# Two of six row groups of a small matrix no longer go through memory

## The chip, the cores and the metric

The kernel runs on one core of a Trainium2 chip. The metric is the device time of one execution in microseconds, the median over several runs.

## The reference

Two kinds of layer alternate, twice each, over an activation `x` of 2048 rows and 640 columns, all in fp32. The first kind is linear attention with 32 heads of 20 columns, the second a dense block with a squared ReLU:

```
qkv = layernorm(x) @ wqkv                       # 640 x 1920
phi(t) = where(t > 0, t + 1, exp(t)) + 1e-6
kv  = einsum("bhsd,bhse->bhde", phi(k), v);  z = sum over s of phi(k)
o   = einsum("bhqd,bhde->bhqe", phi(q), kv) / (einsum("bhqd,bhd->bhq", phi(q), z) + 1e-6)
x   = x + o @ wo
x   = x + relu(layernorm(x) @ w1 + b1)**2 @ w2 + b2     # 640 -> 1728 -> 640
```

## The kernel before

The order of all work on all engines is written out by hand; each engine executes its instructions in that order and waits on semaphores where data is missing. fp32 products are made from three passes over a high and a low half (`split`: ScalarE writes the high half, VectorE the difference), written for the matmuls in the type that the profile shows as fp32r.

A layer has three stages. In the first, the 16 tiles of 128 rows are normalised, transposed and projected to k and q (`part`, matmuls at L416), and G = normalised x times phi(k) is summed up over the tiles. For some tiles the q projection is left over as "late" parts: halves of 320 columns, each 15 matmuls, an exponential on ScalarE (L516) and two operations on VectorE (L523, L524). `late_q(n)` issues n of them. They serve as work for TensorE while other things are made ready.

In the second, short stage, which the change touches, a matrix M of 640 x 640 is made that joins kv and wo, so that the attention's output is phi(q) / den times M. `kv_make` forms the masked block-diagonal kv in six groups of 120 rows (the last of 40). `m_make(c)` multiplies group c by its rows of wo (L967) into a pair of PSUM banks (4, 6 and 2 in turn, from the list `mb`), lets ScalarE copy the 120 x 640 result to a tile `Mc` (L973), and sends that from ScalarE's own DMA queue to a matrix `md` in memory (L974).

M's rows are needed in another order: VectorE transposes q in 32 x 32 blocks only, which leaves the columns of a tile interleaved, and M's rows have to match. Row r of `md`, with r = 160 j + 32 m + b (j below 4, m below 5, b below 32), goes to partition 32 j + b of slice m. Three tiles `m_raw` (named `Mr` in the profile) hold slices 0 and 1, 2 and 3, and 4. `m_read(j, i)` fetches the part of row block j that belongs to tile i, one DMA on SyncE's queue (L979). The table `M_READ` says after which group which reads stand in SyncE's queue: block 0 after group 3, blocks 1 and 2 after group 4, block 3 after group 5. `m_split(m)` then makes the high half of slice m on ScalarE (L1008) and the low half on VectorE (L1009), in the tiles `uM`.

DMAs take eight completion counters in turn, over both issuing queues, so that a DMA is issued only when the one eight before it has landed.

Around this: while the groups are made, VectorE prepares tiles 1 to 3 of phi(q) (`b_step`), and `run_side` takes the next piece from a list of side work, here the splits of these tiles (`b_split`, L145 and L146). After the groups come three late parts, the splits of slices 0 and 1, one side piece, the split of slice 2, a fourth late part, the splits of slices 3 and 4. `proj` (L437) then makes the outputs of the first two tiles: slices 0 to 2 for both, then slices 3 and 4 for both, then tiles 2 and 3. `b_x1` adds the residual on VectorE (L694). SyncE, behind the reads, stores the late parts of phi(q) and loads the first weights of the third stage (L323), the dense block, interleaved with the attention's outputs for the remaining tiles.

Of the kernel before, what the change touches and what calls it, by code (L numbers as in the profile page):

```python
# [10 lines left out]
AF = mybir.ActivationFunctionType  # L11
# [6 lines left out]
DC = D // P  # L18
# [5 lines left out]
B32 = 32  # L24
# [6 lines left out]
NH = -(-D // HR)  # L31
# [21 lines left out]
def fast(b):  # L53
# [13 lines left out]
STAY = 1  # L67
FB0 = 0
KV_STEPS = (0, 1, 1, 1, 1, 0)
M_READ = {  # L70
    3: [(0, i) for i in range(3)],
    4: [(j, i) for i in range(3) for j in (1, 2)],
    5: [(3, i) for i in range(3)],
}
LOW_AT = 1
OUTS = (
# [6 lines left out]
def head_rows(c):  # L83
    return min(HR, D - HR * c)
# [3 lines left out]
def kernel(  # L88
# [11 lines left out]
    nc = tc.nc  # L100
# [13 lines left out]
    def bank(i, n=1):  # L114
        return PS[:, 512 * i : 512 * (i + n)]
# [23 lines left out]
    def ftile(name):  # L139
        return tmp.tile([P, D], F32, tag="f", name=name, bufs=F_BUFS)  # L140
# [265 lines left out]
    def halves(ps):  # L406
        return ps.rearrange("p (b n) -> p b n", b=2)[:, :, :HD]

    def halves_sb(t):
        return t.rearrange("p (b n) -> p b n", b=2)  # L410
# [60 lines left out]
    for layer in range(N_LAYERS):  # L471
# [3 lines left out]
        md = dram.tile([D, D], F32, name=f"md_{layer}", tag="md")  # L475
# [23 lines left out]
        def part(t, a, b, ps=None):  # L499

            ps = (xbank() if ps is None else ps)[:, : b - a]
            for c in range(DC):
                mm3(
                    ps, xT[t][:, 0, c, :], xT[t][:, 1, c, :],
                    kq[c][:, 0, a:b], kq[c][:, 1, a:b], c == 0, c == DC - 1,
                )
            return ps
# [23 lines left out]
        def xtile(name, dtype=R32):  # L531
            return xp.tile([P, 2, D], dtype, tag="x", name=name, bufs=8)
# [23 lines left out]
        if layer == 0:  # L556
# [21 lines left out]
            for ps, a, b in runs:  # L578
# [4 lines left out]
                d = T4[0][:, 0, 0, a * P : b * P]  # L583
                nc.scalar.activation(d, ps[:, : (b - a) * P], AF.Copy)
            first_loads.low(1)
            for ps, a, b in runs:
                d = T4[0][:, 0, :, a * P : b * P]
# [53 lines left out]
        def b_load_x(t):  # L641
            xr[t] = ftile("xr")
            nc.sync.dma_start(xr[t], src[t])
# [31 lines left out]
        def b_step(t, n=1):  # L675
            for _ in range(n):
                next(b_gen.setdefault(t, b_ops(t)), None)
# [7 lines left out]
        def b_split(t, u):  # L685
            split(u[:, 0], u[:, 1], yzp.pop(t))
            pT[t] = chunks(u)
# [51 lines left out]
        for t in range(NT):  # L739
# [66 lines left out]
            ps = ps_first if layer == 0 and t == 1 else part(t, 0, n0, bank(XB[0]))  # L806
# [12 lines left out]
            ps = part(t, n0, D if is_late else 1024, bank(XB[1]))  # L819
# [31 lines left out]
            else:  # L851
                ps = part(t, 1024, 2 * D, bank(XB[2]))
# [21 lines left out]
        def late_q(n=1, rest=True):  # L874

            for _ in range(n):
                if not late_parts:
                    return
                t, j = late_parts.pop(0)
                if j == 0:  # L880
                    late_phi[t] = Phi(ftile("rl"))
                late_phi[t].exp(j * HD, part(t, D + j * HD, D + (j + 1) * HD))
                late_todo.append((t, j))
                if rest:
                    late_rest()
# [21 lines left out]
        for j in range(JB):  # L907
            p, k = slice(j * B32, (j + 1) * B32), j % 2
# [25 lines left out]
        def run_side(n=1):  # L934
            for _ in range(min(n, len(side_work))):
                side_work.pop(0)()
# [3 lines left out]
        u = xtile("kvbd", F32).rearrange("p j n -> p (j n)")  # L940
# [16 lines left out]
                    )  # L957
            nc.vector.tensor_tensor(out=kvbd[c][:n, :n], in0=ps[:n, :n], in1=maskf[:n, :n], op=ALU.mult)

        mb = [4, 6, 2]  # L960

        def m_make(c):
            mb.append(mb.pop(0))
            ps = bank(mb[-1], 2)
            n, o = head_rows(c), HR * c
            for j in range(2):
                nc.tensor.matmul(  # L967
                    ps[:n, j * 512 : j * 512 + HD], kvbd[c][:n, :n],
                    vo["o", c][:n, j * HD : (j + 1) * HD], start=True, stop=True,
                )  # L970

            u = ftile("Mc")
            nc.scalar.activation(halves_sb(u[:n]), halves(ps[:n]), AF.Copy)  # L973
            nc.scalar.dma_start(md[o : o + n], u[:n])  # L974

        def m_read(j, i):

            w = min(2, DC - 2 * i)
            nc.sync.dma_start(  # L979
                m_raw[i][j * B32 : (j + 1) * B32, :w],  # L980
                md[j * R_ + 2 * i * B32 : j * R_ + (2 * i + w) * B32].rearrange(
                    "(m b) n -> b m n", b=B32
                ),
            )
# [21 lines left out]
        def m_split(m):  # L1006
            v = m_raw[m // 2][:, m % 2]
            nc.scalar.activation(M[m][:, 0], v, AF.Copy)  # L1008
            nc.vector.tensor_tensor(  # L1009
                out=M[m][:, 1], in0=v, in1=M[m][:, 0].bitcast(F32), op=ALU.subtract  # L1010
            )

        for c in range(NH):
# [5 lines left out]
            if c == 3:  # L1019
                b_load_x(1)  # L1020
            if KV_STEPS[c]:
                b_step(1, KV_STEPS[c])
        side_work.append(lambda: b_split(1, xtile("pT")))
# [8 lines left out]
        m_raw = [xtile("Mr", F32) for _ in range(3)]  # L1032
        side_work.append(lambda: b_split(2, xtile("pT")))
        Q = (3, 1, 1, 1)
        xbanks = [0, 1, 2, 3]
        for c in range(NH):
            m_make(c)
            b_step(2)
            for j, i in M_READ.get(c, ()):
                m_read(j, i)  # L1040
            if c > 3:
                run_side(1)
            if c > 0:
                b_step(3)
        side_work.append(lambda: b_split(3, xtile("pT")))
        late_q(Q[0])
        for m in range(2):
            m_split(m)
        run_side(1)
        m_split(2)  # L1050
        late_q(1)
        m_split(3)
        m_split(4)
# [89 lines left out]
        def fc1(g, c, spare=False):  # L1143
            if spare:
                ps = fresh("po0")
            elif g == 0 and c == 1:
                ps = fresh("po0")
            else:
                ps = fresh("h")
            u = wu.get(g, "w1", c)  # L1150
            xhi, xlo = xTb[g][:, 0], xTb[g][:, 1]
            if c == 13:
                w = u.rearrange("p (d f) -> p d f", d=DC)
                seq = [(w, xlo), (w, xhi)]
            else:
                w, wl = (u[:, j * D : (j + 1) * D].rearrange("p (d f) -> p d f", d=DC) for j in range(2))
                seq = [(w, xlo), (wl, xhi), (w, xhi)]
            order = [(d, a, bb) for d in range(DC) for a, bb in seq]
            if g == 0 and c == 0:

                order = [(d, a, bb) for a, bb in (seq[1], seq[2], seq[0]) for d in range(DC)]
            for n, (d, a, bb) in enumerate(order):
                nc.tensor.matmul(  # L1163
                    ps, a[:, d, :], bb[:, d, :], start=n == 0, stop=n == len(order) - 1
                )
            wu.used(g, "w1", c)
            return ps
# [425 lines left out]
        for g in range(NG):  # L1593
            for c in range(NF):
                ps = fc1(g, c)
# [63 lines left out]
```

## Time and profile before

| | |
|---|---|
| median of 3 runs | 1347.68 us (1347.3 to 1349.78) |
| profiled execution | 1347.86 us, span 1346.0 us |
| TensorE busy | 1336.2 us, 99% of the span, granted clock 1.0 |
| VectorE, ScalarE busy | 891.5 and 693.6 us (66% and 52%) |
| DMA | 257.32 MB, mean 191 GB/s |

Times in the traces are microseconds from the start of the span. A row of the timeline has start, length, engine, line, operation, tiles (output, then inputs), shapes and count; in brackets stands how long the engine had been idle ahead of it, and what released it. PE is TensorE, PEld its weight loads, ACT ScalarE, DVE VectorE, SPq and ACTq the DMA issues of SyncE and ScalarE. A row of the chain has start, length and what it was; for a DMA the length reaches from issue to landing. A row for a group or a tile ends in count and min/median/max in ns.

Neighbouring matmuls overlap in the pipeline, and their ends are modelled; the pace is read from the starts.

### The profile page before, as it was taken

What the parts mean: (1) busy time and instruction counts of PE and PEld (TensorE: products, weight loads), DVE (VectorE), ACT (ScalarE), POOL (GpSimd) and SP (SyncE); (2) the same over time, 40 slices, a digit from 0 to 9 for tenths busy, and PEclk for the clock granted to TensorE, in tenths of its full rate; (3) what the DMA queues carried; (4) which work ended last, traced back from release to release, by engine and by line L of the source; (5) the groups of instructions that cost most, each with busy time, mean ns of one, the idle gap of its engine ahead of it and who ended that gap; (6) DMA issues with size and microseconds to landing.
All of it is one profiled execution on the core that took longest, in us unless ns stands there. A gap on an engine that the chain in (4) does not pass through costs nothing.

```text
span 1346.0 us, 18739 instructions
## 1 busy us (share of the span) xinstructions
PE 1336.2 (99%) x6746; PEld 1152.8 (86%) x6746; DVE 891.5 (66%) x1601; ACT 693.6 (52%) x1606; POOL 124.1 (9%) x171
## 2 busy tenths in 40 slices
PE   9999999999999999999999999999999999999998
PEld 8888998988888888888888899988888888888887
DVE  8888867877766756543367678678677567665323
ACT  5878843634545426424547686345435535454131
POOL 2222210000000000000012232100000000000000
PEclk9999999999999999999999999999999999999999
DMA  6787837575557475488521115186557565564654
GB/s 205 255 303 268 275 107 236 162 277 174 190 204 230 138 258 184 158 307 296 198 98 53 46 40 156 40 264 239 161 157 273 160 203 188 213 214 143 249 167 156
DMA packets 101296, 257.32 MB, mean 191 GB/s; under 512 B 12884, under 2 KB 37844, under 8 KB 100564
## 3 DMA queue, kind: packets, MB, share of 16 engines
q1 hardware_dynamic: 99610, 252.66, 55.5%
q10 hardware_dynamic: 1594, 3.47, 0.9%
q8 instruction: 53, 0.87, 0.3%
q14 instruction: 39, 0.32, 0.1%
HBM read 196.78 MB, written 59.31 MB: 190 GB/s over the span
## 4 chain that ended last, share of the span: by engine, by line
PE 96%; DMA 2%; ACT 1%; DVE 0%; issue 0%; SPq 0%; DVEq 0%; ACTq 0%
PE PS L416 36%; PE PS L1223 28%; PE PS L1163 28%; PE PS L437 2%; DMA Mr<-md 1%; PE PS L954 1%; PE PS L763 1%; DMA md<-Mc 1%; DMA st<-in_A_wqkv_dram 0%; PE PS L385 0%; ACT Mc L973 0%; ACT uM L1008 0%; ACT pT L145 0%; SPq L979 0%; DVE uM L1009 0%
## 5 line engine op out<-in xcount | busy, mean ns | idle before, releaser
L1163 PE MATMUL PS<-xTb,u 128*128 128x512 f32 x1400 | 332.8, 389 | 0.0
L404 ACT ACTIVATE z<-y 32x160 f32<-32x160 f32 x880 | 294.0, 334 | 59.6 <-DVE y L391 49.6
L1163 PEld LDWEIGHTS PS<-xTb,u 128*128 128x128 f32 x1400 | 262.3, 188 | 53.8
L416 PE MATMUL PS<-kq,xT 128*128 128x320 f32 (+2 forms) x1575 | 283.1, 334 | 0.0
L1223 PE MATMUL PS<-u,h 128*128 128x512 f32 x1120 | 279.6, 390 | 0.0
L416 PEld LDWEIGHTS PS<-kq,xT 128*128 128x128 f32 x1575 | 250.1, 188 | 27.4 <-issue 1.4
L1181 ACT ACTIVATE hr<-PS,b1sb 128x512 f32<-128x512 f32 x104 | 71.5, 687 | 348.3 <-PE PS L1163 346.8
L1223 PEld LDWEIGHTS PS<-u,h 128*128 128x128 f32 x1120 | 208.0, 188 | 39.6
L1185 DVE TENSOR_TENSOR hr<-hr 128x512 f32<-128x512 f32 x104 | 71.3, 685 | 147.3 <-ACT h L1182 147.3
L416 PE MATMUL PS<-kh,xh 128*128 128x512 f32 x480 | 124.1, 392 | 0.0
L516 ACT ACTIVATE e<-PS 128x320 f32<-128x320 f32 (+4 forms) x128 | 53.4, 435 | 110.8 <-PE PS L416 101.6
L375 POOL TENSOR_SCALAR rs<-mv 128x1 f32<-128x1 f32 x63 | 28.8, 457 | 863.1 <-DVE mv L373 863.1
L416 PEld LDWEIGHTS PS<-kh,xh 128*128 128x128 f32 x480 | 87.1, 188 | 15.2 <-DVE kh L727 0.4
L523 DVE TENSOR_SCALAR e<-e 128x320 f32<-128x320 f32 (+4 forms) x128 | 41.5, 324 | 68.8 <-ACT e L516 68.7
L1223 PE MATMUL PS<-h,u 128*128 128x512 f32 x280 | 79.1, 390 | 0.0
L1186 DVE TENSOR_TENSOR h<-hr,h 128x512 fp32r<-128x512 f32 x104 | 72.0, 692 | 7.5
L724 POOL TENSOR_TENSOR acc<-acc,r 128x640 f32<-128x640 f32 x30 | 53.9, 1798 | 197.7 <-DVE r L524 197.7
L1182 ACT ACTIVATE h<-hr 128x512 fp32r<-128x512 f32 x104 | 65.8, 633 | 3.3
L1223 PEld LDWEIGHTS PS<-h,u 128*128 128x128 f32 x280 | 52.0, 188 | 10.5 <-DVE h L1199 0.4
L1431 DVE TENSOR_TENSOR xr<-PS,xr 128x320 f32<-128x320 f32 x48 | 23.5, 489 | 51.5 <-PE PS L416 49.5
L1163 PE MATMUL PS<-xTb,uw 128*128 128x512 f32 x240 | 57.0, 389 | 0.0
L524 DVE SCALAR_TENSOR_TENSOR r<-PS,e 128x512 f32<-128x512 f32 (+2 forms) x104 | 51.1, 491 | 5.8 <-ACT e L516 2.4
(134 smaller groups left out, 1545.6 us busy)
## 6 DMA issues: line engine op xcount, KB each, us to landing
u<-kept_w SPq DMA_DIRECT2D x184, 640.0 KB, 4.8
x<-x SPq DMA_DIRECT2D x48, 320.0 KB, 5.3
kept_w<-uprep SPq DMA_DIRECT2D x23, 640.0 KB, 5.4
pqt<-pq SPq DMA_DIRECT2D x128, 80.0 KB, 4.5
x<-xr SPq DMA_DIRECT2D x32, 320.0 KB, 2.3
st<-in_B_w_dram SPq DMA_DIRECT2D x22, 320.0 KB, 4.2
pq<-r SPq DMA_DIRECT2D x20, 320.0 KB, 2.4
kept_kq<-kq SPq DMA_DIRECT2D x10, 640.0 KB, 6.2
```

What stands on the lines that cost most here:

```text
L404: nc.scalar.activation(d, v, AF.Copy)
L416: nc.tensor.matmul(ps, a, b, start=first and i == 0, stop=last and i == 2)
L516: nc.scalar.activation(self.e[:, a:b], ps, AF.Exp)
L523: nc.vector.tensor_scalar(e, e, 1.0, PHI_EPS, op0=ALU.min, op1=ALU.add)
L524: nc.vector.scalar_tensor_tensor(out=self.r[:, a:b], in0=ps, scalar=0.0, in1=e, op0=ALU.max, op1=ALU.add)
L724: nc.gpsimd.tensor_tensor(out=acc, in0=acc, in1=r, op=ALU.add)
L1163: nc.tensor.matmul(ps, a[:, d, :], bb[:, d, :], start=n == 0, stop=n == len(order) - 1)
L1181: nc.scalar.activation(r, ps, AF.Relu, bias=b1sb[:, c : c + 1])
L1182: nc.scalar.activation(h[:, 0], r, AF.Square)
L1185: nc.vector.tensor_tensor(out=r, in0=r, in1=r, op=ALU.mult)
L1186: nc.vector.tensor_tensor(out=h[:, 1], in0=r, in1=h[:, 0].bitcast(F32), op=ALU.subtract)
L1223: nc.tensor.matmul(ps, l, r, start=first and k == 0, stop=last and k == len(a) - 1)
```

## The change

Only groups 0 to 3 go through `md`. The groups are made in the order 0, 1, 2, 3, 5, 4 with bank pairs 4, 2, 6 in turn. The reads of row block 0 stand after group 2, those of blocks 1 and 2 after group 3 (block 1 first), and block 3 has no reads. Group 5 (40 rows, from row 600) is copied by ScalarE to a tile as before, from which two DMAs on SyncE's queue move 8 rows to slice 3 and 32 rows to slice 4. Group 4 (120 rows, from row 480) starts on a multiple of 32, so ScalarE writes it from PSUM straight to its places, in three copies of 32 rows and one of 24, and no `Mc` tile is taken. The side piece that stood after the fifth group stands after the sixth; the split of slice 2 stands ahead of the next side piece.

```diff
+M_ORDER = (0, 1, 2, 3, 5, 4)
+M_NEAR = (4, 5)
 M_READ = {
-    3: [(0, i) for i in range(3)],
-    4: [(j, i) for i in range(3) for j in (1, 2)],
-    5: [(3, i) for i in range(3)],
+    2: [(0, 0), (0, 1), (0, 2)],
+    3: [(1, 0), (1, 1), (1, 2), (2, 0), (2, 1), (2, 2)],
 }
...
-        mb = [4, 6, 2]
+        mb = [4, 2, 6]
...
-            u = ftile("Mc")
-            nc.scalar.activation(halves_sb(u[:n]), halves(ps[:n]), AF.Copy)
-            nc.scalar.dma_start(md[o : o + n], u[:n])
+            if c not in M_NEAR:
+                u = ftile("Mc")
+                nc.scalar.activation(halves_sb(u[:n]), halves(ps[:n]), AF.Copy)
+                nc.scalar.dma_start(md[o : o + n], u[:n])
+                return
+            near = o % B32 == 0
+            if not near:
+                u = ftile("Mc")
+                nc.scalar.activation(halves_sb(u[:n]), halves(ps[:n]), AF.Copy)
+            r = o
+            while r < o + n:
+                k, b = divmod(r, B32)
+                l = min(B32 - b, o + n - r)
+                j, m = divmod(k, DC)
+                d = m_raw[m // 2][j * B32 + b : j * B32 + b + l, m % 2]
+                if not near:
+                    nc.sync.dma_start(d, u[r - o : r - o + l])
+                else:
+                    nc.scalar.activation(halves_sb(d), halves(ps[r - o : r - o + l]), AF.Copy)
+                r += l
...
-        for c in range(NH):
+        for i, c in enumerate(M_ORDER):
             m_make(c)
             b_step(2)
-            for j, i in M_READ.get(c, ()):
-                m_read(j, i)
-            if c > 3:
+            for r in M_READ.get(c, ()):
+                m_read(*r)
+            if i > 4:
                 run_side(1)
-            if c > 0:
+            if i > 0:
                 b_step(3)
         side_work.append(lambda: b_split(3, xtile("pT")))
         late_q(Q[0])
-        for m in range(2):
+        for m in range(3):
             m_split(m)
         run_side(1)
-        m_split(2)
         late_q(1)
```

## The prediction

> **What bounds the kernel now.** I read the page first: the busy times and the chain that ended last.
>
> ```profile
> PE 1336.2 (99%) x6746; PEld 1152.8 (86%) x6746; DVE 891.5 (66%) x1601; ACT 693.6 (52%) x1606; POOL 124.1 (9%) x171
> PE 96%; DMA 2%; ACT 1%; DVE 0%; issue 0%; SPq 0%; DVEq 0%; ACTq 0%
> ```
>
> TensorE carries the span almost alone. Nothing this change does can be worth more than the few microseconds in which TensorE stands still, so the next view is the list of waits on TensorE.
>
> ```profile
> PE PS L437 <- ACT uM L1008: 3.2, 2, 1.7
> PE PS L437 <- DVE uM L1009: 0.4, 2, 0.2
> ```
>
> Two waits of 3.2 us in total, once in each layer: the first product with M (L437) waits for M's first high half (L1008). That is the place that the change touches. Third, the timeline of it, first layer then second:
>
> ```profile
> 213.29 0.70 ACT L973 ACTIVATE Mc<-PS 120x640 f32<-120x640 f32 x1 [0.45 <-PE PS L967]
> 213.74 9.07 PE L416 MATMUL PS<-kq,xT 128*128 128x320 f32 x60
> 220.65 0.44 ACT L516 ACTIVATE e<-PS 128x320 f32<-128x320 f32 x1 [1.76 <-PE PS L416]
> 221.54 0.49 DVE L524 SCALAR_TENSOR_TENSOR rl<-PS,e 128x320 f32<-128x320 f32 x1
> 223.53 1.37 ACT L1008 ACTIVATE uM<-Mr 128x640 fp32r<-128x640 f32 x2 [2.45 <-DMA Mr<-md]
> 224.30 1.56 DVE L1009 TENSOR_TENSOR uM<-Mr,uM 128x640 fp32r<-128x640 f32 x2 [2.26 <-ACT uM L1008]
> 227.38 11.12 PE L437 MATMUL PS<-uM,pT 128*128 128x320 f32 x74 [0.18 <-DVE uM L1009]
> ...
> 879.34 9.06 PE L416 MATMUL PS<-kq,xT 128*128 128x320 f32 x60
> 886.24 0.44 ACT L516 ACTIVATE e<-PS 128x320 f32<-128x320 f32 x1 [1.76 <-PE PS L416]
> 887.14 0.49 DVE L524 SCALAR_TENSOR_TENSOR rl<-PS,e 128x320 f32<-128x320 f32 x1
> 889.32 1.37 ACT L1008 ACTIVATE uM<-Mr 128x640 fp32r<-128x640 f32 x2 [2.65 <-DMA Mr<-md]
> 893.17 11.12 PE L437 MATMUL PS<-uM,pT 128*128 128x320 f32 x74 [0.18 <-DVE uM L1009]
> ```
>
> TensorE works through four late parts of the q projection (60 matmuls), then has to start 90 products with M. The first 16 stutter behind ScalarE and VectorE, the last 74 run freely. The pace of free matmuls of this size is in the chain:
>
> ```profile
> 240.70 4.40 PE PS L437 x30
> ```
>
> 4.40/30 = 0.147 us. So the 60 late ones are issued by 213.74 + 8.80 = 222.54, the next 16 could be through by 222.54 + 2.35 = 224.89, and the 74 start at 227.38: **2.49 us lost in the first layer**. In the second: 879.34 + 8.80 + 2.35 = 890.49 against 893.17, **2.68 us**. Together 5.17 us, more than the 3.2 us that the wait list shows, because the stutter hides in matmul records. This is the most the change can win there: the order of the work on TensorE is fixed, and nothing of M can be used before 222.54 and 888.14.
>
> **Why M is late.** The fourth view is the DMA queue of SyncE and the chain around it:
>
> ```profile
> 212.87 4.02 DMA md<-Mc
> 216.96 3.99 DMA Mr<-md
> ...
> 875.78 4.71 DMA md<-Mc
> 880.54 3.96 DMA Mr<-md
> ```
>
> ```profile
> 216.96 0.30 SPq L979 DMA_DIRECT2D Mr<-md  x1
> 219.31 0.42 SPq L979 DMA_DIRECT2D Mr<-md  x1
> 881.80 0.42 SPq L979 DMA_DIRECT2D Mr<-md  x1
> 882.51 0.30 SPq L979 DMA_DIRECT2D Mr<-md  x1
> DMA to landing us min/median/max: 3.1/4.0/4.6
> ```
>
> Row block j of M's layout is read back by three DMAs (i = 0, 1, 2). By program order the read issued at 216.96 is (2,0), held for the write of the fourth group, which went out at 212.87 and took 4.02. The one at 219.31 is (3,0), the tenth of twelve, held behind its predecessors in the queue; it is what m_split(0) at 223.53 waits for (4.2 later). In the second layer (2,0) is issued at 882.51.
>
> **The change, part by part.**
>
> *Block 3 no longer through memory.* Two writes and three reads a layer go; ScalarE writes rows 480 to 599 straight from PSUM. What m_split(0) then waits for last is (2,0). In the first layer it is still issued at 216.96, when the fourth group's write has landed; its two predecessors, now (1,1) and (1,2), need only groups two and three, written earlier. It lands at 216.96 + 3.99 = 220.95. In the second layer the order matters: after 881.80 + 0.42 come (1,1) and (1,2), each about 0.45 of queue, and only then (2,0), at about 883.15 instead of 882.51, landing at about 887.15.
>
> *Does that beat TensorE?* The halves take:
>
> ```profile
> L1008 ACT ACTIVATE uM<-Mr x10: 723/725/736, 223.5 to 892.8; 128x640 fp32r<-128x640 f32 x10
> L1009 DVE TENSOR_TENSOR uM<-Mr,uM x10: 815/820/825, 224.3 to 894.6; 128x640 fp32r<-128x640 f32 x10
> ```
>
> Each m takes TensorE 6 matmuls (0.88 us); it needs the high half at the first and the low half at the fifth (0.59 later). First layer: ScalarE is free of the third exponential at 221.09, so high halves of m = 0, 1, 2 are there at 221.85, 222.5, 223.2, wanted at 222.54, 223.42, 224.3. VectorE is free at 222.03, so low halves at 222.85, 223.65, 224.45, wanted at 223.13, 224.0, 224.9. Nothing waits; the least slack is 0.3 us, and (2,0) may land 0.6 us later before anything does. Gain 2.49. Second layer: high halves 887.9, 888.6, 889.2, wanted at 888.14, 889.02, 889.9; low halves 888.75, 889.5, 890.3, wanted at 888.73, 889.6, 890.5. That is level, with no spare: gain 2.68 if the landing takes 4.0, 2.1 if it takes the 4.6 of the row above. I take 2.5.
>
> *Four copies in place of one on ScalarE.* A copy's time hardly depends on its rows (the first fence, copies by shape; the second, what ScalarE does after them):
>
> ```profile
> L973 ACT ACTIVATE Mc<-PS x12: 682/703/705, 208.3 to 881.2; 120x640 f32<-120x640 f32 x10, 40x640 f32<-40x640 f32 x2
> ```
>
> ```profile
> 214.41 0.74 ACT L145 ACTIVATE pT<-z 128x640 fp32r<-128x640 f32 x1 [0.41 <-DVE z L669]
> 216.25 0.44 ACT L516 ACTIVATE e<-PS 128x320 f32<-128x320 f32 x1 [0.51 <-DMA md<-Mc]
> ```
>
> so four of 32 rows cost about 4 x 0.70 = 2.8 us where one cost 0.7. No row shows this shape; the bounds are 4 x 0.682 and, if reading from one quarter into another cost double, 5.6 us. They start when the group at 213.29 is copied (213.97) and the last group's matmuls are through, about 214.2, and end at 217.0. Behind them stand the split of pT (moved past them, 0.74) and the first exponential, which slips from 216.25 to about 217.8. The second and third wait for TensorE anyway (1.76 idle ahead of the third, above), so it is caught up before 220.65: cost nothing. The cover is about 2 us; at 5.6 us for the copies, some 0.8 would reach the halves. The late parts on TensorE wait for none of this: the third needs the bank pair of the 40-row group, copied by 214, and the products with M need the last pair at 225.
>
> *Two moves from tile to tile on SyncE* (8 and 32 rows) come last in its queue, at about 218.2 and 218.7, second layer 884.95 and 885.4. The nearest rows are the reads: they land 3.1 to 4.6 later, the longest at 890.0. m_split(3) has its turn on ScalarE only after three halves, a pT split and an exponential, at 224.3 and 890.3, and TensorE wants m = 3 after 36 products (5.29 us) at 227.83 and 893.43. Cost nothing, with over 3 us of cover beyond the longest landing. The Trainium skill, page "DMA: Bandwidth & Descriptors", section "Anatomy of one DMA", puts most of a DMA's fixed 2 us on the receipt of the write, heaviest towards HBM, on the software path; by its formula 80 KB would land in an estimated 2.2 us. No run here shows a tile-to-tile move; by it the sum is the same and the cover two microseconds larger, so that the rival of late moves, below, would have half its chance.
>
> *Behind the moves* SyncE has the pq stores and the first weights; they come a microsecond or two earlier. *Bank order 4, 2, 6*: the second group now waits for the mask multiply of the sixth kv:
>
> ```profile
> 206.97 6.84 PE L967 MATMUL PS<-uraw,kvbd 120*120 120x320 f32 x24
> 207.53 0.15 DVE L958 TENSOR_TENSOR kvbd<-PS,mask 40x40 f32<-40x40 f32 x1
> ```
>
> It is done at 207.68, and TensorE, at 6.84/6 = 1.14 us a group, gets there at 208.1: nothing.
>
> *What is late next.* The products end 2.5 us earlier; VectorE must be there for the residual:
>
> ```profile
> 229.54 2.06 DVE L996 TENSOR_TENSOR Mr<-Mr 128x320 f32<-128x320 f32 x4
> 232.38 0.82 DVE L694 TENSOR_TENSOR xr<-PS,xr 128x640 f32<-128x640 f32 x1 [0.77 <-PE PS L437]
> ```
>
> From its first low half to the end of L996 VectorE took 224.30 to 231.60, 7.3 us. Begun at 222.03 that ends at 229.33, and L694 is wanted at 232.38 - 2.49 = 229.89: 0.5 to spare, in the second layer 0.25. From there on the chain is TensorE without a break, and all work moves with it. I take 0.1 us a layer for it.
>
> **The sum.** 2.49 + 2.5 - 0.2 = 4.8 us off the profiled execution's 1347.86 (span 1346.0). That execution is 0.18 above the median of 1347.68; against the median the forecast is **1342.9 us**. 0.2% is 2.7 us, about what a measurement of this kernel can tell from no change.
>
> **Rivals.**
> - *The reads of block 2 become the bound.* Their landing, not block 3, was already the chain in the first layer, and the second layer is level. The longest landing of any transfer of this matrix is that of a write:
>
> ```profile
> DMA to landing us min/median/max: 2.9/4.0/5.2
> ```
>
>   If the reads took 5.2, the loss is 0.6 and 1.2: a gain of 3.2, 1344.5. Only from 5.5 does it fall below 2.7 us. For it: the write of 4.71 in the second layer. Against: two writes and three reads fewer share the engines.
> - *No change.* Another wait takes the whole place: VectorE late at the residual, or the ScalarE copies at twice their price holding up the halves. Each priced above at under 1 us a layer, so both and more are needed: 1347.
> - *Slower: the moves.* A transfer issued among weight loads can be very late:
>
> ```profile
> u<-kept_w SPq DMA_DIRECT2D x6, 640.0 KB, 7.6
> pqt<-pq SPq DMA_DIRECT2D x1, 80.0 KB, 12.2
> ```
>
> At 12.2 the move for m = 3 lands at 230.4 and 897.15, its high half is there 0.72 later, and TensorE stands 3.3 and 4.4 us where it now loses 2.49 and 2.68: 0.8 + 1.7, and with VectorE and the residuals behind it about 3 us slower, 1351. It decides from a landing of about 11 us. Against: the moves go out ahead of the weights on the same queue.
> - *That it doesn't do what it says:* the built program holds the four writes, the two moves and nine reads a layer, so no chance for this.
>
> **The chances.** Forecast (a gain of 4 to 5.4) 0.70; reads as the bound 0.16, of which most is still over 2.7; no change 0.08; slower 0.06. So faster 0.82, within 0.2% 0.13, slower 0.05. The low end is the full 5.17 with 0.7 for the spread of the runs (1347.3 to 1349.78): 1341.8. The high end takes in the reads as bound in both layers and half of the no-change case: 1346.0.
>
> **What would show it.** In the profile after, the wait of L437 on the high halves is gone or under 0.3 us, 90 products with M run in one piece from about 222.6 and 888.2, the first high half starts near 221.1 and 887.2, and the four copies take about 2.8 us ending before 217.5. The forecast is wrong if a wait on M is still there, released by a DMA (reads or moves) or by VectorE's low halves, or if TensorE stalls between the products and the first layer of the feed-forward stage.

## The result, and the profile after

The changed kernel takes 1342.93 us (median of 7, 1342.6 to 1345.11) against 1347.68 (median of 7, 1347.24 to 1349.78): 4.75 us less. The ratio is 0.9964, with a 95% interval from 0.9952 to 0.9975. Run once more beside the kernel before it took 1343.19 against 1347.76, ratio 0.9965 (0.9952 to 0.9977). The forecast was 1342.9.

The page of after, the same two lines as before:

```profile
PE 1336.0 (99%) x6746; PEld 1154.6 (86%) x6746; DVE 891.5 (66%) x1601; ACT 697.8 (52%) x1612; POOL 124.2 (9%) x171
PE 99%; DMA 0%; ACT 0%; SPq 0%; DVE 0%; DVEq 0%; issue 0%
```

TensorE does the same 6746 matmuls in the same busy time; DMA went from 2% of the chain to nothing, and ScalarE has 4.2 us more work. The list of TensorE's waits:

```profile
PE PS L766 <- ACT xT L587: 1.4, 1, 1.4
PE PS L565 <- POOL ident masks.py:199: 1.4, 1, 1.4
PE PS L583 <- DVE xt L580: 0.3, 1, 0.3
```

All three lie in the first microseconds of the kernel; no wait on M is left. The timeline around M, first layer, then second (m_make's matmuls are L970 now, the copies into place L993, the moves L991, the halves L1028 and L1029, the products L440, the residual L697):

```profile
209.09 7.03 PE L970 MATMUL PS<-uraw,kvbd 120*120 120x320 f32 x24
215.72 9.21 PE L419 MATMUL PS<-kq,xT 128*128 128x320 f32 x60
216.17 2.85 ACT L993 ACTIVATE Mr<-PS 32x640 f32<-32x640 f32 x4
220.34 1.39 SPq L991 DMA_DIRECT2D Mr<-Mc  x2
223.10 1.98 ACT L1028 ACTIVATE uM<-Mr 128x640 fp32r<-128x640 f32 x3
224.77 13.36 PE L440 MATMUL PS<-uM,pT 128*128 128x320 f32 x90
232.01 0.82 DVE L697 TENSOR_TENSOR xr<-PS,xr 128x640 f32<-128x640 f32 x1 [0.63 <-PE PS L440]
...
878.89 9.21 PE L419 MATMUL PS<-kq,xT 128*128 128x320 f32 x60
886.74 1.99 ACT L1028 ACTIVATE uM<-Mr 128x640 fp32r<-128x640 f32 x3 [0.36 <-DMA Mr<-md]
887.51 2.30 DVE L1029 TENSOR_TENSOR uM<-Mr,uM 128x640 fp32r<-128x640 f32 x3 [0.18 <-ACT uM L1028]
895.17 0.82 DVE L697 TENSOR_TENSOR xr<-PS,xr 128x640 f32<-128x640 f32 x1 [0.35 <-PE PS L440]
```

Where 16 products stuttered and 74 ran, 90 run in one piece, and they begin as the late parts end. The first layer's times are 2.1 us late here, in the slowest execution of the seven. Two pieces of each chain, before and then after, show that it comes from the first microseconds of the kernel: 44 matmuls start 0.76 us later, and they take 1.38 us longer:

```profile
1.71 4.98 DMA st<-in_A_wqkv_dram
7.78 6.88 PE PS L763 x44
```

```profile
1.69 5.77 DMA st<-in_A_wqkv_dram
8.54 8.26 PE PS L766 x44
```

The longer time of the 44 is a fall of TensorE's granted clock: it was 0.50 from 8.7 to 12.1 us here and 1.00 in the same stretch of before. The last section comes back to such falls.

So that layers can be compared over executions, I take the length of the second stage: from the first of m_make's matmuls to the first matmul of the dense block, by the starts in each timeline. Before: 206.97 to 255.31 and 872.57 to 921.12. These are the lengths in all kernels of this study, with the median times. The lengths are those of each kernel's profiled execution; the last column is the median of the kernel before, run beside it:

| kernel | layer one | layer two | median us | before, beside it |
|---|---|---|---|---|
| before | 48.34 | 48.55 | 1347.68 | |
| after | 45.91 | 45.90 | 1342.93 | 1347.68 |
| after, once more | 45.92 | 45.91 | 1343.19 | 1347.76 |
| ordering edits alone | 49.56 | 48.16 | 1348.41 | 1347.76 |
| places alone | 46.06 | 46.17 | 1343.13 | 1347.76 |
| before, five late parts ahead of M | 47.14 | 46.71 | 1345.47 | 1347.76 |
| group 4 by four moves | 47.24 | 47.41 | 1345.54 | 1347.26 |
| copies issued twice | 47.33 | 49.57 | 1345.98 | 1347.26 |
| weights ahead of the moves | 47.91 | 48.53 | 1347.27 | 1347.26 |
| three late parts ahead of M, one later | 53.19 | 53.05 | 1357.62 | 1347.26 |
| three late parts ahead of M, one last | 46.89 | 49.41 | 1345.68 | 1347.85 |
| reads of block 2 earlier | 45.92 | 45.92 | 1342.41 | 1347.85 |

### The profile page after: what moved, and what is told of

Its sections match the earlier page's. It is cut to its first block, busy times and chain, and to the rows that moved or that the text cites. A ratio compares the mean times of both kernels' runs of the same rounds, so it can differ in the third digit from the quotient of the medians.

```text
span 1343.2 us, 18730 instructions
## 1 busy us (share of the span) xinstructions
PE 1336.0 (99%) x6746; PEld 1154.6 (86%) x6746; DVE 891.5 (66%) x1601; ACT 697.8 (52%) x1612; POOL 124.2 (9%) x171
## 4 chain that ended last, share of the span: by engine, by line
PE 99%; DMA 0%; ACT 0%; SPq 0%; DVE 0%; DVEq 0%; issue 0%
PE PS L419 38%; PE PS L1242 28%; PE PS L1182 28%; PE PS L440 3%; PE PS L970 1%; PE PS L957 1%; PE PS L766 1%; DMA st<-in_A_wqkv_dram 0%; PE PS L388 0%; PE PS L907 0%; PE PS L1282 0%; ACT kq L205 0%; DVE x L1293 0%; SPq L227 0%; SPq L457 0%; DVEq L1673 0%
```

## The experiments

**The changed kernel once more**, for a profile with an ordinary start.

> The changed kernel once more, for a profile whose start is like that of before: in the profiled execution of after the first loads landed later and the second stage of layer one began 2.1 us late. Theory: with the start alike, the second stage ends 2.4 us earlier in the first layer and 2.6 more in the second, and the span is 1341 us, the time 1342.9. Rival (the late start belongs to the change): the second stage begins at 209.1 again.

The second stage began at 207.08, as before the change (206.97), and the span was 1341.2. The late start does not belong to the change.

**The ordering edits alone**: bank pairs, side piece and split of slice 2. The groups are still made in the order 0 to 5.

```diff
-        mb = [4, 6, 2]
+        mb = [4, 2, 6]
...
-            if c > 3:
+            if c > 4:
                 run_side(1)
...
-        for m in range(2):
+        for m in range(3):
             m_split(m)
         run_side(1)
-        m_split(2)
```

> The kernel before with the ordering edits alone: bank pairs 4, 2, 6, the side piece after the sixth group, the split of slice 2 ahead of the next side piece. All six groups still go through memory. Theory (the last read from memory sets when M can be used): the first high half still waits for the read of row block 3, so the wait on it stays at 1.5 to 1.7 us a layer; only the stutter after it shortens, since slice 2 is split one ScalarE piece earlier, about 0.5 us a layer: 1346.7 us. Rival (the order of the work, not the way of the rows, makes the gain): the wait falls under 0.5 us and the time to 1343 to 1344.

1348.41 against 1347.76, ratio 1.0001 (0.9992 to 1.001): no gain. TensorE's wait on M stood as before:

```profile
PE PS L437 <- ACT uM L1008: 3.4, 2, 1.8
```

The rival falls. The half microsecond a layer that I expected is there in the second layer (48.16 against 48.55) and not in the first: behind the wait the granted clock fell there, which cost 1.7 us (last section), and without these the length would be 47.85 against 48.34.

**The places alone**: group 4 and 5 as in the change, all ordering edits undone.

```diff
-M_ORDER = (0, 1, 2, 3, 5, 4)
+M_ORDER = (0, 1, 2, 3, 4, 5)
...
-        mb = [4, 2, 6]
+        mb = [4, 6, 2]
...
-            if i > 4:
+            if i > 3:
                 run_side(1)
...
-        for m in range(3):
+        for m in range(2):
             m_split(m)
         run_side(1)
+        m_split(2)
```

> The changed kernel with the ordering edits undone: groups made in the order 0 to 5, bank pairs 4, 6, 2, the side piece after the fifth group, slice 2 split after the side piece; groups 4 and 5 still do not go through memory. Theory: M's first halves are in time as in the changed kernel; slice 2's low half comes one piece later, about 225.2 where TensorE wants it at 224.9 on the first layer's clock of before, a stutter of 0.3 to 0.8 us a layer: 1343.5 to 1344.5 us. Rival (order makes the gain): 1347.

1343.13, ratio 0.9968 (0.9957 to 0.998). The way of the rows carries the gain: 2.28 and 2.38 us of stage length of the 2.42 and 2.64. The ordering edits, the order of the groups among them, add 0.14 and 0.26, which the times don't show (1343.19 with them). I had put 0.3 to 0.8 a layer on slice 2's low half coming later; it was less, and 0.14 of it comes from another place: with the 40-row group fifth and not last, the late parts begin 6.63 us after the stage's start, with the natural order 6.78.

One order was not tried: all groups through memory, with block 3's first read ahead of the other blocks' later reads. In the first layer of before it could win nothing, since that read went out at 219.31 and the write of group 4, issued at 214.03, took 5.2 us to land. In the second layer that write, issued at 880.16, landed after 3.6 us, and the read went out at 885.79, 2 us later. A part of the second layer's gain might be had so; it is not shown.

**Group 4 by moves**: one copy to a tile and four more DMAs, in place of four copies.

```diff
-            near = o % B32 == 0
+            near = False
```

> The changed kernel, with group 4 also copied once to a tile and moved from there to its places by four DMAs on SyncE's queue, in place of the four copies by ScalarE. Theory: ScalarE is relieved of 2.1 us that cost nothing, and six moves stand in SyncE's queue where there were two; the one for slice 0 is issued about 1.4 us after the first move of after and lands 2.9 us later, at 224.6 on the clock of the trace of after where ScalarE began the first half at 223.1, and at 888.3 where it began at 886.7. TensorE waits 1.1 and 1.3 us: 1345.3 us. Rival (the copies by ScalarE held something up): 1342 or less.

1345.54, where 1345.3 was expected. The first line is from TensorE's wait list, the others are ScalarE's timeline:

```profile
PE PS L440 <- ACT uM L1028: 1.7, 2, 0.9
```

```profile
223.25 1.99 ACT L1028 ACTIVATE uM<-Mr 128x640 fp32r<-128x640 f32 x3 [1.71 <-DMA Mr<-Mc]
887.95 2.00 ACT L1028 ACTIVATE uM<-Mr 128x640 fp32r<-128x640 f32 x3 [1.88 <-DMA Mr<-Mc]
```

The 2.1 us that ScalarE saves a layer buy nothing: it stands idle for 1.71 and 1.88 us ahead of the halves. The six moves, one behind the other in SyncE's queue, bring half of M's wait back, and 2.8 us of stage length with it. What the copies give is that the rows are in place early.

**The copies twice**, each of the four issued a second time.

```diff
-                    nc.scalar.activation(halves_sb(d), halves(ps[r - o : r - o + l]), AF.Copy)
+                    for _ in range(2):
+                        nc.scalar.activation(halves_sb(d), halves(ps[r - o : r - o + l]), AF.Copy)
```

> The changed kernel with each of the four copies into place issued twice, 2.85 us more on ScalarE a layer. The prediction's reading: about 2 us of this is covered, 0.8 reaches the high halves, 1344.5 us. Reading from the trace of after: VectorE comes out worse than ScalarE, since the split of pT and three exponentials' rests stand ahead of the first low half; it ends at 226.6 where TensorE wants it at 225.1: 1.5 us a layer, 1345.9 us. Rival (ScalarE has slack in plenty): 1342.9.

1345.98: 3 us more than the changed kernel, 1345.9 by the reading from the trace, 1344.5 by the prediction. TensorE waits for VectorE (the edit adds a line, so the halves are L1029 and L1030):

```profile
PE PS L440 <- DVE uM L1030: 2.5, 2, 1.3
PE PS L440 <- ACT uM L1029: 0.2, 1, 0.2
```

VectorE's own rows in the first layer, the low part of pT's split and M's first low halves:

```profile
220.25 0.83 DVE L149 TENSOR_TENSOR pT<-z,pT 128x640 fp32r<-128x640 f32 x1 [3.96 <-ACT pT L148]
223.35 2.29 DVE L1030 TENSOR_TENSOR uM<-Mr,uM 128x640 fp32r<-128x640 f32 x3
```

**Weights ahead of the moves.**

```diff
             for r in M_READ.get(c, ()):
                 m_read(*r)
+            if c == 3:
+                wu.free = 3
+                wu.load_ring()
...
-        wu.free = 3
-        wu.load_ring()
```

> The changed kernel with the first three weight loads (640 KB each) ahead of the two moves in SyncE's queue, where they stood behind. Theory (the moves have over 3 us of cover, and the weights take 5.8 to 8.8 us to land): the moves land 7 us after issue, about when slice 3's turn comes; TensorE waits under 1 us: 1343 to 1344.5 us. Rival (the prediction's slower case: a small transfer behind weights takes 12 us): slice 3 comes 4 to 5 us late in each layer, 1350 to 1352 us.

1347.27 against 1347.26, ratio 1.0 (0.9992 to 1.0009): the whole gain is gone, and the time lies between the two expectations. Two pieces of the chain, ScalarE's high halves of slices 3 and 4 in both layers, and TensorE's waits:

```profile
220.66 7.72 DMA Mr<-Mc
885.12 8.28 DMA Mr<-Mc
```

```profile
227.54 1.60 ACT L1028 ACTIVATE uM<-Mr 128x640 fp32r<-128x640 f32 x2 [3.63 <-DMA Mr<-Mc]
893.48 1.36 ACT L1028 ACTIVATE uM<-Mr 128x640 fp32r<-128x640 f32 x2 [4.22 <-DMA Mr<-Mc]
```

```profile
PE PS L419 <- DVE xr L697: 2.2, 2, 1.1
PE PS L440 <- ACT uM L1028: 1.2, 2, 1.0
```

Behind three loads of 640 KB the 80 KB move landed after 7.7 us in the first layer instead of 2.8, and a move in the second after 8.3. TensorE waited 0.24 and 0.99 us for slice 3, and then once more, 1.15 and 1.03 us, for the residual of tile 2 to free its bank. VectorE's queue made that second wait. Its rows in the first layer:

```profile
228.31 1.69 DVE L1029 TENSOR_TENSOR uM<-Mr,uM 128x640 fp32r<-128x640 f32 x2 [2.50 <-ACT uM L1028]
229.92 2.06 DVE L1016 TENSOR_TENSOR Mr<-Mr 128x320 f32<-128x320 f32 x4
231.90 0.82 DVE L697 TENSOR_TENSOR xr<-PS,xr 128x640 f32<-128x640 f32 x1
```

The low halves of slices 3 and 4 start 2.6 us later after the stage's start than in the second run of after (3.3 in the second layer). They and the four operations of L1016 stand ahead of the first residual, so VectorE no longer idles there, and the residual comes 2.0 and 2.6 us late.

**One more late part ahead of M, in the kernel before.**

```diff
-        Q = (3, 1, 1, 1)
+        Q = (4, 1, 1, 1)
```

> The kernel before, with one more late part (15 matmuls, 2.2 us) ahead of the products with M, so that five stand there in place of four; the last late part, between the last transposes and the dense block, is gone for it. Theory (TensorE only lacked work while M was on its way): the wait on M goes, but the filler is missing ahead of the dense block, where the last tile's high half comes about 0.9 us after TensorE wants it: a gain of 1.6 us a layer, 1344.5 us. Rival 1 (the wait simply returns in the other place): 1347.7. Rival 2 (filler was in excess there, and the change was not needed): 1342.9.

1345.47, ratio 0.9981 (0.9972 to 0.999), about half of the change's gain; the theory's 1344.5 was a microsecond too good. The wait on M shrinks to 0.2 us, and a new one stands ahead of the dense block:

```profile
PE PS L1163 <- ACT xTb L145: 1.6, 2, 0.8
PE PS L437 <- DVE uM L1009: 0.2, 1, 0.2
```

So M's wait could be filled with other work, but the filler is missed elsewhere. For the rest of the gain M had to come earlier.

**One late part fewer ahead of M, in the changed kernel**, to see how early M is.

```diff
-        Q = (3, 1, 1, 1)
+        Q = (2, 2, 1, 1)
```

> The changed kernel with one late part fewer (15 matmuls, 2.2 us) ahead of the products with M, done after tile 2's output instead, so that TensorE wants M 2.2 us earlier. It measures how early M really is. Theory (M is ready 0.3 to 0.7 us ahead of its use): TensorE waits 1.1 to 1.5 us in the first layer and about 2 in the second, and the work put later fills nothing: 1346 to 1347 us. Rival (M is ready well ahead and the cover is large): 1342.9 us.

1357.62, 11 us beyond what either theory allowed. The waits on M were shorter than expected, 0.44 and 1.35 us; the rest was my own making. Done after tile 2's output, the second late part needs the bank that this output stands in. The timeline, and TensorE's granted clock (the number behind the engines' counts) in two stretches:

```profile
241.33 4.37 PE L419 MATMUL PS<-kq,xT 128*128 128x320 f32 x15 [4.25 <-DVE xr L697]
```

```profile
230.00:236.00 6.00, 6.00 (x43) 6.00 (x42) 4.68 (x11) 2.54 (x8) 1.52 (x4) 1.00 1.02 412
241.00:243.00 2.00, 1.67 (x6) 1.67 (x7) 1.73 (x5) 0.26 (x1) 0.39 (x2) 0.50 0.03 8
```

4.25 us of wait a layer, and behind it 15 matmuls in 4.37 us, where the chain of before has such 15 in 2.20. To keep this apart from M, the part went to the very end:

```diff
-        Q = (3, 1, 1, 1)
+        Q = (2, 1, 1, 1)
```

> The changed kernel with one late part fewer ahead of the products with M, as in the run with two late parts, but that part is done last, behind the transposes and ahead of the dense block, not after tile 2's output. In the earlier run TensorE waited 0.44 and 1.35 us for M and then 4.25 us in each layer for the PSUM bank that the second late part needed (freed by the residual of tile 2). Theory: without that bank wait only the waits on M are left, 0.44 and 1.35 us and a stutter of some 0.4 in each layer, and the late part ahead of the dense block fills something: 1344.5 to 1346 us, clock near 1. Rival (the excess of that run came from asking for M early): 1355 us or more.

1345.68, as expected, with the waits on M alone:

```profile
PE PS L440 <- ACT uM L1028: 2.0, 2, 1.5
```

The products begin 14.1 and 15.1 us after the stage's start, as early as M's reads allow; in the changed kernel TensorE comes to them at 15.67. The reads leave 1.5 us in the first layer and about 0.6 in the second. In the changed kernel itself a third exponential stands ahead of the first high half on ScalarE, which in the first layer starts 14.01 us after the stage's start and takes 0.73: there the high half is 0.9 us early.

**The reads of block 2 two places earlier.**

```diff
-    3: [(1, 0), (1, 1), (1, 2), (2, 0), (2, 1), (2, 2)],
+    3: [(1, 0), (2, 0), (1, 1), (2, 1), (1, 2), (2, 2)],
```

> The changed kernel with the reads after the fourth group in the order (1,0), (2,0), (1,1), (2,1), (1,2), (2,2), so that the read that the first split waits for is issued two places earlier. The prediction called the second layer level, with no spare for a late landing. Theory (TensorE has no wait on M left): no change, 1342.9 to 1343.3 us. Rival (the split of slice 0 still comes too late in some executions): 1342.5 us or less.

1342.41, ratio 0.9956 (0.9944 to 0.9969), against 0.9965 for the changed kernel on another chip; the intervals overlap. By the number this is the rival's range, but the stage is 45.92 us in both layers, as without the edit, and the stage in the first layer began at 206.36 instead of 207.08: the difference lies ahead of the edit's place. No effect shown, so no version here is shown to beat the changed kernel.

## Why the prediction was right

*The bound: 2.49 + 2.68 us in which TensorE lacked M.* The stage became 2.42 and 2.64 us shorter (before against the second run of after), 5.06 together, and no wait on M is left. From the start of the late parts, without the 0.14 us that the order of the groups gave, it is 2.28 and 2.50, together 4.78. The sum was 4.8; the medians differ by 4.75, and by 4.57 in the second run. That the hit is so exact is luck: six of the seven executions of after lie within half a microsecond and the seventh 2 us above, the order of the groups was not in the sum, and a part of the sum was not needed (VectorE, below).

*Block 2 becomes the last read.* Right in the second layer, where ScalarE is released by a read from memory, 0.36 us after it was free. In the first the exponential ends at about 223.1 and the half starts at once, so the read had landed. "Level, with no spare" was close: the first high half starts at 886.74 and is there at 887.47, wanted at 878.89 + 8.80 = 887.69. In the second run of after no half waited for a read in either layer.

*Four copies at 0.70.* They took 2.85 us and ended 9.9 us after the stage's start, 217.0 - 206.97 = 10.0 predicted. The upper bound, double, did not occur. That they cost nothing in the changed kernel is shown by TensorE's wait list, which has no wait in this stage. **The cover was mis-sized**: I reckoned it on ScalarE, "about 2 us", with 0.8 us reaching the halves if the copies took double. Doubled, they cost 1.4 and 3.7 us of stage length in the profiled execution, 1.7 of the 3.7 through a fall of the clock, and 3 us by the medians. The tighter cover is VectorE's: its low part of pT's split waits for ScalarE, and three late parts' rests stand behind that and ahead of M's first low half.

*The moves.* Predicted at 218.2, 11.2 us after the stage's start; issued at 220.34, 11.25 after it. The 80 KB one landed in 2.8 us in the second run of after and 2.9 in the first, below the reads' 3.1 of before. The Trainium skill, page "DMA: Bandwidth & Descriptors", section "Anatomy of one DMA", gives the formula of the estimate of 2.2, for the software path; on SyncE's queue here it was too low by 0.6 to 0.7. One step failed, the point for the slower rival, "a landing of about 11 us". With the weights ahead the moves went out 1.5 us later and slice 3 was there about 9.2 and 9.8 us after the moves' place in the changed kernel, and the gain was already gone. I had counted up to TensorE's want of slice 3 and put the chain behind it, "VectorE and the residuals", into half a microsecond; it cost 2.2 us by the wait list. The mechanism of that rival is real, and what kept it away is the place of the moves ahead of the weights.

*VectorE at the residual*: 0.5 and 0.25 us to spare were predicted; it sits idle 0.63 and 0.35 us ahead of L697, so the 0.1 us a layer that the sum took off for it was not lost.

*The rivals.* Reads as the bound: landings of this matrix ran to 4.4 us in after, and none cost TensorE anything. That order makes the gain: excluded by the ordering edits alone and, for the order of the groups, by the places alone.

## What to carry to other kernels

Where one engine carries the span, count the work that it could have issued, not the waits that the list shows: the listed waits for M were 3.6 us of the 5.17 lost, the rest was stutter behind them, and the sum of both was nearly the gain. Cover for a step that is moved has to be followed through every engine's queue that stands behind it, here VectorE's behind ScalarE's and the residual chain behind the products; the smallest cover decides, and twice it was not on the engine that the edit touched. Filler work moved to a gap is missed where it came from: half of the gain was to be had so, the whole only by having the data earlier.

## What the runs showed of the hardware

A wait can cost more than its length, though not in every execution. In the profile of the ordering edits alone, TensorE waited 1.61 us for M in the first layer, about as long as before; then its granted clock was 0.68 for the next 3 us and 0.75 for another 3:

```profile
222.20:224.00 1.80, 0.19 (x3) 0.04 (x1) 0.06 (x1) 0.83 (x2) 0.00 (x0) 1.00 0.99 334
224.00:227.00 3.00, 3.00 (x13) 2.73 (x14) 3.00 (x5) 3.00 (x6) 0.00 (x0) 0.68 1.05 260
227.00:230.00 3.00, 3.00 (x18) 3.00 (x17) 2.88 (x6) 0.36 (x1) 0.00 (x0) 0.75 0.93 369
```

The same stretch of before had its wait of 1.51 us and a clock of 1.00:

```profile
224.00:227.00 3.00, 2.68 (x16) 2.35 (x16) 2.70 (x4) 3.00 (x7) 0.00 (x0) 1.00 1.01 273
```

The lost share of 0.32 and 0.25 over 3 us each is 1.7 us. A closer stretch shows what it is, half the clock for 3.4 us:

```profile
223.96:225.11 1.15, 1.15 (x6) 0.88 (x7) 1.15 (x2) 1.15 (x3) 0.00 (x0) 1.00 1.10 230
225.12:228.52 3.40, 3.40 (x15) 3.40 (x14) 3.31 (x7) 2.24 (x5) 0.00 (x0) 0.50 0.94 303
228.53:230.00 1.47, 1.47 (x12) 1.47 (x12) 1.44 (x3) 0.00 (x0) 0.00 (x0) 1.00 1.01 398
```

The second layer of the doubled copies (49.57 in the table, a wait of 1.34 us) and of the run with one late part last (49.41, 1.49 us) show the same 3.4 us at half clock, and so does the start of the first run of after, behind a wait of 1.42 us. After the waits of 4.25 us it came in both layers of the profiled execution, for 6.8 us in the first; all five executions of that kernel have a mean clock of 0.995 to 0.997. No such fall stands behind the waits of 1.51 and 1.71 us in before.

The Trainium skill, page "TensorE: Matmul & The Clock Gate", section "Part 1: The HAM clock gate", lets the clock fall to half after an idle window of about 3.4 us. In the waits of 4.25 us the clock fell to half 2.6 and 3.7 us after they began, which is near that window; but waits of less than half of it were enough in some executions here.

Of the 64 executions of before that ran beside the experiments, 12 have a mean clock of 0.998 or less and take 1348.4 to 1350.6 us; of the 12 of the changed kernel none has, nor of the 11 of the other two kernels without a wait on M (places alone, reads of block 2 earlier). The mean is a coarse sign: it reads 0.999 for the execution of after with the fall at its start. So removing this wait seems to remove a risk as well, which the prediction did not count. Why the clock falls in one execution and not in the next, these runs don't show.
